# 128-wide stationary reads, a new row order with one store per 128-token tile, and smaller steps in a fused attention and token-mixer kernel

## The chip, the cores and the metric

One core of one Trainium2 chip. The metric is the device time of one execution in microseconds (us). A run is called "slow" when it is over 1.5% above the fastest of its kernel, and the other "fast". A profile is one execution; its span is about 1.8 us shorter than the time of the same run. In the profile PE is TensorE's matmul, PEld its weight load, DVE VectorE, ACT ScalarE, POOL GpSimd, and SP or SyncE the engine that issues most DMAs (93 of 107 before).

## The reference

```python
# q, k, v: (8 batches, 8 heads, 576 tokens, 64); p: (8, 8, 32, 64); fp32 in and out
p_packed = softmax(p @ k.T / 8) @ v               # 32 packed rows a head
x        = softmax(q @ p_packed.T / 8) @ p_packed  # (8, 576, 512) once the heads are side by side
wq, wk   = x @ w_q, x @ w_k                        # (576, 64) each
mixed    = (wq @ wk.T / 8) @ x
out      = relu(mixed) @ w_out                     # (8, 576, 512)
```

## The kernel before

It never builds x: everything after the softmax works with the 512 columns of softmax weights, and each batch goes through 24 kinds of step (transposes of k and q, scores, softmax, `at`, `wk`, `wq`, `g`, `y`, `mx`, `oa`/`ob`). A table of times, `TIMES`, is sorted to give one fixed order of all steps of all batches; each engine runs its part of it in that order. A batch's 576 tokens are token = s * 18 + j, with s from 0 to 31 and j from 0 to 17.

The parts that matter (cuts marked):

```python
def rows(name, b):            # q: partition = (head, s), free = j: 18 tokens next to each other
    ...

def qc(b, c):                 # chunk c takes every third pair of j: j = 6 r + 2 c + x
    ... x_in["q", b].rearrange("a G (r c x) d -> a c G r (x d)", c=NC3, x=2)[:, c]

def sc(b, c):                 # scores: 96 query rows are the stationary operand
    for h in range(H):
        nc.tensor.matmul(ps[:, :, h, :], qT[:, h].rearrange("a r s -> a (r s)"),
                         st[b]["ppT"][:, h], start=True, stop=True)

def wk(b, c):                 # 96 columns of aT are the stationary operand
    ...

def pq(b, _):                 # the first time, it casts the weights itself (DVE and ACT, half each)
    if b == 0:
        for i in range(2):
            copy(i, wqk[:, :, i * Dl:(i + 1) * Dl], w_first[:, :, i * Dl:(i + 1) * Dl])
    ...

def store(b, t0, o):          # a tile of 128 tokens crosses the 96-row pieces: 2 stores a tile
    o_v = out[b].rearrange("(n m) d -> m n d", m=QR)      # QR = 6
    t, end = t0, t0 + o.shape[0]
    while t < end:
        m, n = t // CH, t % CH                            # CH = 96
        k = min(CH - n, end - t)
        nc.sync.dma_start(o_v[m, n:n + k], o[t - t0:t - t0 + k])
        t += k
```

A batch has four tiles of 128 tokens; the last 64 tokens of two batches make up a fifth tile (the "rest").

The softmax here doesn't subtract the row's maximum and nothing guards it: scores larger than these inputs give would overflow.

Of the kernel before, what the change touches and what calls it, by code (L numbers as in the profile page):

```python
# [10 lines left out]
def kernel(  # L11
# [8 lines left out]
    moe_w_out: bass.AP,  # L20
    out: bass.AP,
):



# [10 lines left out]
    nc = tc.nc  # L36
# [21 lines left out]
    NF = KG * RK // NC3  # L58
    NT = NF // 2
    CH = S // (2 * NC3)  # L60
    QR = R // NC3
    VW = Dh + 2
    SM = S // P * P
# [2 lines left out]

    TIMES = (
        (13.00, {
            "lk": (-19.68,),
            "lv": (-16.69,),  # L70
            "lq": (-10.53,),
            "kc": (-1.65, -1.61, -2.24),
            "qc": (4.73, 7.19, 6.10),
            "vc": (1.43, 0.22, 2.76),
            "kt": (0.00, 0.69, 1.45),
            "sa": (1.33, 3.59, 4.04),
            "pv": (6.00,),
            "pb": (23.74,),
            "pt": (8.67,),
            "pq": (16.55,),  # L80
            "qt": (7.33, 11.66, 9.31),
            "sc": (10.66, 13.24, 11.68),
            "sm": (12.44, 14.97, 13.37),
            "at": (18.48, 19.75, 17.43),
            "wk": (20.20, 21.45, 20.93),
            "wq": (22.14, 24.72),
            "g": (22.73,),
            "y": (25.15,),
            "pr": (8.86,),
        }),  # L90
        (13.09, {
            "mx": (30.23, 30.57, 30.04, 33.47, 27.08),
            "oa": (47.09, 37.92, 40.87, 38.92, 43.80),
            "ob": (48.10, 39.32, 41.98, 41.94, 44.92),
        }),
    )

    dve_relu = (0, 1, 0, 0)
    dve_wk = (0, 0, 1)
    dve_wq = (1, 0)  # L100
    dve_out = (0, 0, 1, 0, 0)
    act_kc = (0, 0, 1)
    act_qc = (1, 1, 0)
    act_vc = (0, 0, 1)
    dve_g, dve_y = 1, 0
    def pool(name, bufs, psum=False):
# [10 lines left out]
    def psum(pl, shape, dt, name):  # L117
        return pl.tile(shape, dt, tag="ps", name=name)
# [16 lines left out]
    def load(name, b, pieces=None):  # L135

        x_in[name, b] = t = two.tile(shape[name], fp32, tag=name + "_in", name=name + "_in")
        for o in pieces or [slice(None)]:
            nc.sync.dma_start(t[o], rows(name, b)[o])  # L139
# [17 lines left out]
    wqk = const.tile([Dh, H, 2 * Dl], bf16)  # L157
    wout_w = const.tile([P, NJ, D], bf16)
    ident = const.tile([P, P], bf16)
    w_first = const.tile([Dh, H, 2 * Dl], fp32)  # L160
    warm = const.tile([P, 512], bf16)

    nc.sync.dma_start(p_first, p_v[:, 0])
    by_head = [(slice(None), G) for G in range(KG)]
    load("k", 0, by_head)
    load("v", 0, by_head)
    load("q", 0)
    for i, w in enumerate((moe_w_q, moe_w_k)):
        nc.sync.dma_start(w_first[:, :, i * Dl:(i + 1) * Dl],
                          w.rearrange("(h d) c -> d h c", d=Dh))  # L170
    for name in "kvq":
        load(name, 1)

# [18 lines left out]
    def constants():  # L192
        nc.vector.memset(warm, 0.0)  # L193
        make_identity(nc, ident)
        nc.vector.memset(pT[:, 0:2], 0.0)
        for t in v_bufs:
            nc.vector.memset(t[:, :, Dh:], 1.0)
        for t in ppT_bufs:
            nc.vector.memset(t, 0.0)
        nc.gpsimd.memset(mask, 0.0)  # L200
        for pos in range(NP):
            nc.gpsimd.memset(mask[pos * L:(pos + 1) * L, pos, :], 1.0)
        for t in g_bufs:
            nc.gpsimd.memset(t, 0.0)
        nc.gpsimd.memset(pT[:, 2:], 0.0)
        nc.vector.tensor_copy(
            perm, ident[0:CH, 0:CH].rearrange("a (r sh) -> a sh r", sh=QP))

    def warm_up(n):

        ps = psum(w_pool, [P, 512], fp32, "warm_ps")
        for i in range(n):
            nc.tensor.matmul(ps, warm[:, 0:P], warm, start=True, stop=True)  # L213

    perm = const.tile([CH, QP, NC3], bf16)
    ppT_bufs = [const.tile([P, H, 2, L], bf16, name=f"ppT{i}") for i in range(2)]
    g_bufs = [const.tile([P, NG, P], bf16, name=f"g_sb{i}") for i in range(2)]
    mask = const.tile([P, NP, Dh], fp32)


    st = [{} for _ in range(B)]
# [21 lines left out]
    def qc(b, c):  # L243

        if b < NL:
            st[b]["q", c] = t = three.tile([P, NG, NC3, 2, Dh], bf16, tag="q_c", name="q_c")
            cast(act_qc[c], t.rearrange("a G r x d -> a G r (x d)"),
                 x_in["q", b].rearrange("a G (r c x) d -> a c G r (x d)", c=NC3, x=2)[:, c])

    def kt(b, c):  # L250
        xk = st[b]["k", c] if b < NL else flat(x_in["k", b], c)
# [54 lines left out]
                 ps[r].rearrange("a G (pos l) -> a (G pos) l", l=L))  # L306

    def pq(b, _):
        if b == 0:
            for i in range(2):  # L310
                copy(i, wqk[:, :, i * Dl:(i + 1) * Dl], w_first[:, :, i * Dl:(i + 1) * Dl])
        ps = psum(w_pool, [P, NG, 2 * Dl], fp32, "pqk_ps")
        for h in range(H):
            G, pos = h // NP, h % NP
            nc.tensor.matmul(ps[pos * L:(pos + 1) * L, G, :], st[b]["ppT"][0:Dh, h, 0, :],  # L315
                             wqk[:, h, :], start=True, stop=True)
        st[b]["pqk"] = pqk = three.tile([P, NG, 2 * Dl], bf16, tag="pqk", name="pqk")
        nc.scalar.activation(pqk, ps, COPY)

    def qt(b, c):  # L320
        xq = (st[b]["q", c] if b < NL else
              x_in["q", b].rearrange("a G (r c x) d -> a c G r x d", c=NC3, x=2)[:, c])
        ps = transposes([xq[:, G, r].rearrange("a x d -> a (x d)")
                         for r in range(NC3) for G in range(NG)])
        st[b]["qT", c] = qT = four.tile([P, H, NC3, QP], bf16, tag="qT", name="qT")
        nc.vector.tensor_copy(qT, ps.rearrange("a (r G) (pos s) -> a (G pos) r s", G=NG, s=QP))  # L326

    def sc(b, c):
        qT = st[b]["qT", c]
        ps = psum(sc_pool, [CH, 2, H, L], fp32, "e2_ps")  # L330
        for h in range(H):
            nc.tensor.matmul(ps[:, :, h, :], qT[:, h].rearrange("a r s -> a (r s)"),  # L332
                             st[b]["ppT"][:, h], start=True, stop=True)
        st[b]["e2", c] = e2 = four.tile([CH, 2 * H, L], fp32, tag="e2", name="e2")
        nc.scalar.activation(e2.rearrange("a (x h) l -> a x h l", x=2), ps, EXP, scale=scale)

    def sm(b, c):
        e2 = st[b]["e2", c]
# [6 lines left out]
        st[b]["a2", c] = a2.rearrange("a (x G pos) l -> a x G (pos l)", x=2, G=NG)  # L345

    def at(b, c):
        if "aT" not in st[b]:
            st[b]["aT"] = three.tile([P, NG, NC3, 2, CH], bf16, tag="aT", name="aT")
        ps = psum(tp_pool, [P, NG, 2, CH], bf16, "aT_ps")  # L350
        for par in range(2):
            for G in range(NG):
                nc.tensor.transpose(ps[:, G, par, :], st[b]["a2", c][:, par, G, :],  # L353
                                    perm.rearrange("a s r -> a (s r)"))
        nc.vector.tensor_copy(st[b]["aT"][:, :, c], ps)  # L355

    def wk(b, c):
        ps = psum(w_pool, [CH, 2, Dl], fp32, "wk_ps")
        for par in range(2):
            for G in range(NG):  # L360
                nc.tensor.matmul(ps[:, par, :], st[b]["aT"][:, G, c, par, :],  # L361
                                 st[b]["pqk"][:, G, Dl:], start=G == 0, stop=G == NG - 1)
        st[b]["wk", c] = t = six.tile([CH, 2, Dl], bf16, tag="wk", name="wk")
        copy(dve_wk[c], t, ps)

    def wq(b, half):
        if "wqT" not in st[b]:
            st[b]["wqT"] = four.tile([P, S], bf16, tag="wqT", name="wqT")
        hs = slice(half * S // 2, (half + 1) * S // 2)
        ps = psum(w_pool, [P, S // 2], fp32, "wq_ps")  # L370
        for G in range(NG):
            nc.tensor.matmul(ps, st[b]["pqk"][:, G, :],  # L372
                             st[b]["aT"][:, G].rearrange("a c x s -> a (c x s)")[:, hs],
                             start=G == 0, stop=G == NG - 1)
        if dve_wq[half]:
            nc.vector.tensor_scalar_mul(st[b]["wqT"][:, hs], ps, scale2)
        else:
            nc.scalar.activation(st[b]["wqT"][:, hs], ps, COPY, scale=scale2)

    def g(b, _):  # L380
        ps = psum(w_pool, [P, NG, Dl], fp32, "g_ps")
# [41 lines left out]

    def store(b, t0, o):

        o_v = out[b].rearrange("(n m) d -> m n d", m=QR)
        t, end = t0, t0 + o.shape[0]
        while t < end:
            m, n = t // CH, t % CH
            k = min(CH - n, end - t)  # L430
            nc.sync.dma_start(o_v[m, n:n + k], o[t - t0:t - t0 + k])
            t += k

    def o_half(b, c, half):

# [34 lines left out]
    def lq(b, _):  # L470
        if b >= NL:
            load_cast("q", b)
        if b == NL:
            nc.gpsimd.dma_start(wout_w, moe_w_out.rearrange("(j r) c -> r j c", r=P))

    def pr(b, _):
        if b % 2 == 1 and b + 1 < B:
            p_transposes((b + 1) // 2)

    steps = dict(lk=lk, lv=lv, lq=lq, kc=kc, qc=qc, vc=vc, kt=kt, sa=sa, pv=pv, pb=pb, pt=pt, pq=pq, qt=qt,  # L480
                 sc=sc, sm=sm, at=at, wk=wk, wq=wq, g=g, y=y, mx=mx, oa=oa, ob=ob, pr=pr)
    todo = sorted((t + b * period, b, name, c)
                  for period, times in TIMES for name, ts in times.items()
                  for c, t in enumerate(ts) for b in range(B))
# [40 lines left out]
```

## Time and profile before

| | before |
|---|---|
| time, median of the first 3 runs (range) | 134.47 us (133.61 to 134.76) |
| span of the profiled run | 130.9 us |
| g matmuls of batches 0 to 7 start at | 33.0, 43.9, 56.2, 68.8, 81.2, 93.8, 105.6, 114.8 us |
| start of last matmul to end of span | 6.2 us |
| stores | 72 |

The g matmuls come once a batch; their times are read from the starts of matmuls in the trace.

From the page of the kernel before: busy time of the engines, then the span in 40 slices of 3.3 us (busy tenths of PE; PEclk, the granted clock in tenths; DMA, the mean busy share of 16 DMA engines; GB/s), then the chain of work that ended last, by engine and by line.

```profile
span 130.9 us, 4877 instructions
...
PE 116.0 (89%) x2040; PEld 78.6 (60%) x2040; DVE 80.8 (62%) x198; ACT 86.1 (66%) x176; POOL 67.8 (52%) x90
...
PE   5796299499996999999999999999999999999920
...
PEclk9999859959999999999999999999999999999995
DMA  4999999999999999799999999999953431765784
GB/s 131 323 362 365 262 387 353 322 288 287 275 248 229 343 219 239 121 232 266 406 252 216 291 400 255 201 366 351 189 163 88 111 118 37 222 165 122 227 240 133
...
PE 77%; DMA 7%; ACT 3%; SPq 3%; DVE 2%; issue 2%; POOL 1%; ACTq 0%
PE out_ps L444 24%; PE T_ps L228 12%; DMA q_in<-in_q_dram 7%; PE e_ps L332 7%; PE warm_ps L213 5%; PE mix_ps L413 5%; PE e_ps L265 4%; PE aT_ps L353 4%; PE wk_ps L361 3%; PE pv_ps L280 3%; PE wq_ps L372 3%; SPq L139 3%; PE g_ps L385 2%; PE y_ps L394 1%; PE pqk_ps L315 1%
```

PE is busy to 9 tenths in nearly every slice from the ninth to the 38th, and 77% of the chain is PE. The DMA digits are 9 until slice 29 (but for the first slice and one 7) and then fall: most loads are done by then.

The windows view of a stretch in the middle (length, then busy time and count of each engine, clock, DMA share, GB/s):

```profile
core 0: us, PE busy (x) PEld busy (x) DVE busy (x) ACT busy (x) POOL busy (x), PEclk, DMA share, GB/s
...
61.60:74.00 12.40, 12.40 (x249) 8.99 (x247) 9.53 (x23) 9.67 (x22) 7.25 (x10) 1.00 1.09 290
...
```

PE is busy for all of the stretch and the others for 58 to 78% of it.

Groups of instructions (line, engine, operation, operands, shape, count | busy us, mean ns of one | idle time of the engine before them, and its releaser):

```profile
L124 ACT ACTIVATE o_sb<-out_ps 128x512 f32<-128x512 f32 x28 | 16.7, 595 | 7.7 <-PE out_ps L444 6.0 <-ACT wk L124 0.6 <-DMA out_dram<-o_sb 0.6
...
L332 PEld LDWEIGHTS <-qT 128*96 128x96 bf16 x192 | 11.6, 128 | 1.3 <-issue 0.2
L444 PEld LDWEIGHTS <-relu 128*128 128x128 bf16 x128 | 11.2, 99 | 7.4 <-issue 0.4
...
L361 PEld LDWEIGHTS <-aT 128*96 128x96 bf16 x96 | 7.0, 124 | 2.2 <-DVE aT L355 0.2
```

A weight load of 96 columns takes 128 or 124 ns and one of 128 columns 99 ns, although it loads more.

DMA issues of stores (out, in, queue, count, KB each, median us from issue to landing):

```profile
out_dram<-o_sb SPq DMA_DIRECT2D x24, 192.0 KB, 3.7
...
out_dram<-o_sb SPq DMA_DIRECT2D x24, 64.0 KB, 3.4
```

They land in 3.4 to 3.7 us (medians) for 64 to 192 KB. Two lines of the timeline of the end (start, duration, engine, what):

```profile
118.08 10.21 SPq L431 DMA_DIRECT2D out_dram<-o_sb  x18
...
125.20 0.60 ACT L124 ACTIVATE o_sb<-out_ps 128x512 f32<-128x512 f32 x1 [0.31 <-PE out_ps L444]
```

SyncE issues the last 18 stores back to back until 128.3 us, while the last tile is copied at 125.2 to 125.8.

### The profile page before, as it was taken

To read this page: it belongs to the slowest core of one execution; us is meant where nothing else is said; L and a number is where in the kernel's file an instruction comes from. 1 tells how busy PE (TensorE), PEld (TensorE's weight loads), DVE (VectorE), ACT (ScalarE), POOL (GpSimd) and SP (SyncE) were. 2 spreads that over 40 slices of the span, in tenths; PEclk is the share of its full clock that TensorE was granted. 3 is DMA by queue.
4 is the path that set the end of the run, shared out by engine and by line. 5 is a ranking of instruction groups with operands and counts; after the bars stand their busy time and mean duration, and the time that the engine had idled before them with its cause. 6 is when DMAs were issued, how large, how long until landed. Compare 5 with 4: busy or idle time off the path is not lost.

```text
span 130.9 us, 4877 instructions
## 1 busy us (share of the span) xinstructions
PE 116.0 (89%) x2040; PEld 78.6 (60%) x2040; DVE 80.8 (62%) x198; ACT 86.1 (66%) x176; POOL 67.8 (52%) x90
## 2 busy tenths in 40 slices
PE   5796299499996999999999999999999999999920
PEld 1253277257864975786678677767876785654400
DVE  6150049526796877878777887887688777524200
ACT  3144426572794689588867877696789678858530
POOL 7924527994099268709841982388048408400000
PEclk9999859959999999999999999999999999999995
DMA  4999999999999999799999999999953431765784
GB/s 131 323 362 365 262 387 353 322 288 287 275 248 229 343 219 239 121 232 266 406 252 216 291 400 255 201 366 351 189 163 88 111 118 37 222 165 122 227 240 133
DMA packets 18630, 32.10 MB, mean 245 GB/s; under 512 B 2736, under 2 KB 6832, under 8 KB 18608
## 3 DMA queue, kind: packets, MB, share of 16 engines
q1 hardware_dynamic: 12880, 23.99, 55.1%
q0 software_dynamic: 5728, 7.80, 35.4%
q8 instruction: 16, 0.26, 0.8%
q14 instruction: 6, 0.05, 0.1%
HBM read 30.15 MB, written 9.44 MB: 302 GB/s over the span
## 4 chain that ended last, share of the span: by engine, by line
PE 77%; DMA 7%; ACT 3%; SPq 3%; DVE 2%; issue 2%; POOL 1%; ACTq 0%
PE out_ps L444 24%; PE T_ps L228 12%; DMA q_in<-in_q_dram 7%; PE e_ps L332 7%; PE warm_ps L213 5%; PE mix_ps L413 5%; PE e_ps L265 4%; PE aT_ps L353 4%; PE wk_ps L361 3%; PE pv_ps L280 3%; PE wq_ps L372 3%; SPq L139 3%; PE g_ps L385 2%; PE y_ps L394 1%; PE pqk_ps L315 1%
## 5 line engine op out<-in xcount | busy, mean ns | idle before, releaser
L444 PE MATMUL out_ps<-wout_w,relu 128*128 128x512 bf16 x128 | 33.9, 379 | 0.0
L124 ACT ACTIVATE o_sb<-out_ps 128x512 f32<-128x512 f32 x28 | 16.7, 595 | 7.7 <-PE out_ps L444 6.0
L326 DVE COPY qT<-T_ps 128x768 bf16<-128x768 bf16 x24 | 13.3, 555 | 9.7 <-PE T_ps L228 9.3
L213 PE MATMUL warm_ps<-warm 128*128 128x512 bf16 x40 | 17.5, 472 | 1.2 <-DVE warm L193 1.2
L255 DVE COPY kT<-T_ps 128x768 bf16<-128x768 bf16 x24 | 13.0, 546 | 6.7 <-PE T_ps L228 5.7
L444 PEld LDWEIGHTS <-relu 128*128 128x128 bf16 x128 | 11.2, 99 | 7.4 <-issue 0.4
L404 ACT ACTIVATE relu<-mix_ps 128x512 bf16<-128x512 f32 x24 | 13.5, 604 | 2.7 <-PE mix_ps L413 2.4
L332 PEld LDWEIGHTS <-qT 128*96 128x96 bf16 x192 | 11.6, 128 | 1.3 <-issue 0.2
L355 DVE COPY aT<-aT_ps 128x384 bf16<-128x384 bf16 x24 | 8.5, 353 | 6.2 <-PE aT_ps L353 6.2
L413 PE MATMUL mix_ps<-wqT,y 128*128 128x512 bf16 x32 | 10.6, 381 | 0.1
L294 POOL TENSOR_TENSOR ppb<-pp,mask 128x256 bf16<-128x256 bf16 x16 | 10.5, 676 | 0.1
L228 PE MATMUL T_ps<-ident,q_bf 128*128 128x128 bf16 x108 | 9.1, 219 | 1.1 <-issue 1.1
L122 DVE COPY o_sb<-out_ps 128x512 f32<-128x512 f32 x8 | 5.4, 671 | 7.1 <-PE out_ps L444 3.7
L228 PE MATMUL T_ps<-ident,k_bf 128*128 128x128 bf16 x108 | 9.0, 219 | 0.0
L265 PE MATMUL e_ps<-pT,kT 128*64 128x64 bf16 x288 | 8.3, 201 | 0.2 <-DVE kT L255 0.2
L228 PEld LDWEIGHTS <-k_bf 128*128 128x128 bf16 x108 | 7.0, 98 | 2.2
L361 PEld LDWEIGHTS <-aT 128*96 128x96 bf16 x96 | 7.0, 124 | 2.2 <-DVE aT L355 0.2
L124 ACT ACTIVATE wk<-wk_ps 96x128 bf16<-96x128 f32 x16 | 4.3, 270 | 6.0 <-PE wk_ps L361 6.0
L228 PEld LDWEIGHTS <-q_bf 128*128 128x128 bf16 x108 | 7.0, 100 | 2.0 <-issue 1.5
L265 PEld LDWEIGHTS <-kT 128*64 128x64 bf16 x288 | 6.2, 113 | 3.3 <-DVE kT L255 1.1
L361 PE MATMUL wk_ps<-pqk,aT 128*96 128x64 bf16 x96 | 7.7, 207 | 0.0
L342 DVE RECIPROCAL rr<-rs 96x16 f32<-96x16 f32 x24 | 6.0, 249 | 1.8
(320 smaller groups left out, 272.2 us busy)
## 6 DMA issues: line engine op xcount, KB each, us to landing
v_in<-in_v_dram SPq DMA_DIRECT2D x7, 1152.0 KB, 10.0
out_dram<-o_sb SPq DMA_DIRECT2D x24, 192.0 KB, 3.7
k_bf<-in_k_dram POOLq DMA_DIRECT2D x6, 576.0 KB, 11.7
q_bf<-in_q_dram POOLq DMA_DIRECT2D x6, 576.0 KB, 8.2
out_dram<-o_sb SPq DMA_DIRECT2D x24, 128.0 KB, 3.5
q_in<-in_q_dram SPq DMA_DIRECT2D x2, 1152.0 KB, 12.8
out_dram<-o_sb SPq DMA_DIRECT2D x24, 64.0 KB, 3.4
k_in<-in_k_dram SPq DMA_DIRECT2D x4, 288.0 KB, 3.7
```

The lines of the kernel that those rows point to most:

```text
L124: nc.scalar.activation(o, i, COPY)
L213: nc.tensor.matmul(ps, warm[:, 0:P], warm, start=True, stop=True)
L228: nc.tensor.transpose(ps[:, t, :], block, ident)
L255: nc.vector.tensor_copy(kT, ps)
L265: nc.tensor.matmul(ps[m, t], kT[:, t, m], heads[:, 2 * h0:2 * h1 + 2:2 * (h1 - h0) + 1], start=True, stop=True)
L294: nc.gpsimd.tensor_tensor(ppb[:, G], st[b]["pp"][:, G, 0:1, :].to_broadcast((P, NP, Dh)), mask, op=MULT)
L326: nc.vector.tensor_copy(qT, ps.rearrange("a (r G) (pos s) -> a (G pos) r s", G=NG, s=QP))
L332: nc.tensor.matmul(ps[:, :, h, :], qT[:, h].rearrange("a r s -> a (r s)"), st[b]["ppT"][:, h], start=True, stop=True)
L361: nc.tensor.matmul(ps[:, par, :], st[b]["aT"][:, G, c, par, :], st[b]["pqk"][:, G, Dl:], start=G == 0, stop=G == NG - 1)
L404: nc.scalar.activation(o, i, RELU)
L413: nc.tensor.matmul(ps, yT[:, j * P:(j + 1) * P], wqT[:, 0:SM], start=True, stop=True)
L444: nc.tensor.matmul(ps, lhsT, wout_w[:, j, :], start=j == 0, stop=j == NJ - 1)
```

## The change

Its intent: read the weights of scores and wk 128 wide (the 32 columns too many belong to the next head or a zero pad, and their results are never read), so that the load takes the 99 ns of a 128-column one and not 124 to 128; choose rows so that 128 tokens of out are one regular DMA; make wq per chunk, so that it needn't wait for a half; cast the small weights as steps of their own, and load them before q. The order of steps was fitted anew.

```diff
-            cast(... x_in["q", b].rearrange("a G (r c x) d -> a c G r (x d)", c=NC3, x=2)[:, c])
+            cast(... x_in["q", b].rearrange("a G (c r x) d -> a c G r (x d)", c=NC3, x=2)[:, c])
# scores, and wk in the same way; qT and aT become fixed buffers with a zero pad of 32 columns
-        ps = psum(sc_pool, [CH, 2, H, L], fp32, "e2_ps")
+        ps = psum(sc_pool, [P, 2, H, L], fp32, "e2_ps")
         for h in range(H):
-            nc.tensor.matmul(ps[:, :, h, :], qT[:, h].rearrange("a r s -> a (r s)"),
+            nc.tensor.matmul(ps[:, :, h, :], qT[:, h * CH:h * CH + P],
                              st[b]["ppT"][:, h], start=True, stop=True)
# wq: 3 chunks of 192 columns in place of 2 halves of 288; all on ACT; one more relu on DVE
# weights: loaded into output buffers before q, and cast in steps "wc" on ACT; q of batch 0 in 3 loads
     def store(b, t0, o):
-        o_v = out[b].rearrange("(n m) d -> m n d", m=QR)
-        t, end = t0, t0 + o.shape[0]
-        while t < end:
-            m, n = t // CH, t % CH
-            k = min(CH - n, end - t)
-            nc.sync.dma_start(o_v[m, n:n + k], o[t - t0:t - t0 + k])
-            t += k
+        n = o.shape[0] // QP                                      # QP = 32
+        nc.sync.dma_start(
+            out[b].rearrange("(s j) d -> j s d", j=R)[t0 // QP:t0 // QP + n],   # R = 18
+            o)
# ... (TIMES, the engine of each eviction and of some casts, and the operand of the warm-up matmuls changed too)
```

More of the change, by code (lines that the diff above doesn't have):

```diff
@@ L60 @@
     CH = S // (2 * NC3)
+    PAD = P - CH
     QR = R // NC3
@@ L68 @@
         (13.00, {
-            "lk": (-19.68,),
-            "lv": (-16.69,),
-            "lq": (-10.53,),
-            "kc": (-1.65, -1.61, -2.24),
-            "qc": (4.73, 7.19, 6.10),
-            "vc": (1.43, 0.22, 2.76),
-            "kt": (0.00, 0.69, 1.45),
-            "sa": (1.33, 3.59, 4.04),
-            "pv": (6.00,),
-            "pb": (23.74,),
-            "pt": (8.67,),
-            "pq": (16.55,),
-            "qt": (7.33, 11.66, 9.31),
-            "sc": (10.66, 13.24, 11.68),
-            "sm": (12.44, 14.97, 13.37),
-            "at": (18.48, 19.75, 17.43),
-            "wk": (20.20, 21.45, 20.93),
-            "wq": (22.14, 24.72),
-            "g": (22.73,),
-            "y": (25.15,),
-            "pr": (8.86,),
-        }),
-        (13.09, {
-            "mx": (30.23, 30.57, 30.04, 33.47, 27.08),
-            "oa": (47.09, 37.92, 40.87, 38.92, 43.80),
-            "ob": (48.10, 39.32, 41.98, 41.94, 44.92),
+            "lk": (-20.02,),
+            "lv": (-16.79,),
+            "lq": (-9.81,),
+            "kc": (-3.51, -0.84, -2.25),
+            "qc": (5.53, 6.68, 5.38),
+            "vc": (-0.49, 2.31, 2.35),
+            "kt": (0.00, 1.68, 1.54),
+            "sa": (1.39, 3.02, 2.92),
+            "pv": (5.79,),
+            "pb": (23.13,),
+            "pt": (7.81,),
+            "pq": (14.00,),
+            "qt": (9.65, 10.22, 6.81),
+            "sc": (12.18, 12.94, 9.66),
+            "sm": (13.07, 15.48, 12.14),
+            "at": (18.57, 19.72, 16.97),
+            "wk": (19.93, 22.49, 20.85),
+            "wq": (22.64, 25.47, 25.97),
+            "g": (23.46,),
+            "y": (26.35,),
+            "pr": (9.83,),
+            "wc": (9.00, 9.50),
+        }),
+        (13.11, {
+            "mx": (29.53, 29.32, 29.98, 28.93, 35.84),
+            "oa": (46.33, 41.06, 42.47, 39.49, 43.39),
+            "ob": (48.09, 41.28, 42.65, 41.28, 44.75),
         }),
     )
-    dve_relu = (0, 1, 0, 0)
+    dve_relu = (0, 1, 0, 1)
     dve_wk = (0, 0, 1)
-    dve_wq = (1, 0)
+    dve_wq = (0, 0, 0)
     dve_out = (0, 0, 1, 0, 0)
-    act_kc = (0, 0, 1)
-    act_qc = (1, 1, 0)
+    act_kc = (0, 1, 0)
+    act_qc = (0, 1, 1)
     act_vc = (0, 0, 1)
@@ L159 @@
     ident = const.tile([P, P], bf16)
-    w_first = const.tile([Dh, H, 2 * Dl], fp32)
-    warm = const.tile([P, 512], bf16)
+    warm = const.tile([P, P], bf16)
     nc.sync.dma_start(p_first, p_v[:, 0])
@@ L166 @@
     load("v", 0, by_head)
-    load("q", 0)
+    w_first = []
     for i, w in enumerate((moe_w_q, moe_w_k)):
-        nc.sync.dma_start(w_first[:, :, i * Dl:(i + 1) * Dl],
-                          w.rearrange("(h d) c -> d h c", d=Dh))
+        t = opool.tile([P, D], fp32, tag="o", name="w_first")[0:Dh].rearrange(
+            "a (h c) -> a h c", c=Dl)
+        nc.sync.dma_start(t, w.rearrange("(h d) c -> d h c", d=Dh))
+        w_first.append(t)
+    load("q", 0, [(slice(None), slice(None), slice(c * QR, (c + 1) * QR)) for c in range(NC3)])
     for name in "kvq":
@@ L205, in constants @@
         nc.gpsimd.memset(pT[:, 2:], 0.0)
-        nc.vector.tensor_copy(
-            perm, ident[0:CH, 0:CH].rearrange("a (r sh) -> a sh r", sh=QP))
+        for t in qT_bufs:
+            nc.vector.memset(t[:, H * CH:], 0.0)
+        for t in aT_bufs:
+            nc.vector.memset(t[:, :, NG * CH:], 0.0)
     def warm_up(n):
@@ L212, in warm_up @@
         for i in range(n):
-            nc.tensor.matmul(ps, warm[:, 0:P], warm, start=True, stop=True)
-    perm = const.tile([CH, QP, NC3], bf16)
+            nc.tensor.matmul(ps.rearrange("a (x n) -> a x n", n=P), warm,
+                             warm.unsqueeze(1).to_broadcast((P, 4, P)), start=True, stop=True)
+    qT_bufs = [const.tile([P, H * CH + PAD], bf16, name=f"qT{i}") for i in range(4)]
+    aT_bufs = [const.tile([P, 2 * NC3, NG * CH + PAD], bf16, name=f"aT{i}") for i in range(3)]
     ppT_bufs = [const.tile([P, H, 2, L], bf16, name=f"ppT{i}") for i in range(2)]
@@ L218 @@
     mask = const.tile([P, NP, Dh], fp32)
+    qt_order = sorted(range(NC3), key=lambda c: TIMES[0][1]["qt"][c])
+    qt_order = [qt_order.index(c) for c in range(NC3)]
     st = [{} for _ in range(B)]
@@ L247, in qc @@
             cast(act_qc[c], t.rearrange("a G r x d -> a G r (x d)"),
-                 x_in["q", b].rearrange("a G (r c x) d -> a c G r (x d)", c=NC3, x=2)[:, c])
+                 x_in["q", b].rearrange("a G (c r x) d -> a c G r (x d)", c=NC3, x=2)[:, c])
     def kt(b, c):
@@ L308, in pq @@
     def pq(b, _):
-        if b == 0:
-            for i in range(2):
-                copy(i, wqk[:, :, i * Dl:(i + 1) * Dl], w_first[:, :, i * Dl:(i + 1) * Dl])
         ps = psum(w_pool, [P, NG, 2 * Dl], fp32, "pqk_ps")
@@ L321, in qt @@
         xq = (st[b]["q", c] if b < NL else
-              x_in["q", b].rearrange("a G (r c x) d -> a c G r x d", c=NC3, x=2)[:, c])
+              x_in["q", b].rearrange("a G (c r x) d -> a c G r x d", c=NC3, x=2)[:, c])
         ps = transposes([xq[:, G, r].rearrange("a x d -> a (x d)")
                          for r in range(NC3) for G in range(NG)])
-        st[b]["qT", c] = qT = four.tile([P, H, NC3, QP], bf16, tag="qT", name="qT")
-        nc.vector.tensor_copy(qT, ps.rearrange("a (r G) (pos s) -> a (G pos) r s", G=NG, s=QP))
+        st[b]["qT", c] = qT = qT_bufs[(NC3 * b + qt_order[c]) % 4]
+        nc.vector.tensor_copy(
+            qT[:, 0:H * CH].rearrange("a (h r s) -> a h r s", r=NC3, s=QP),
+            ps.rearrange("a (r G) (pos s) -> a (G pos) r s", G=NG, s=QP))
     def sc(b, c):
         qT = st[b]["qT", c]
-        ps = psum(sc_pool, [CH, 2, H, L], fp32, "e2_ps")
+        ps = psum(sc_pool, [P, 2, H, L], fp32, "e2_ps")
         for h in range(H):
-            nc.tensor.matmul(ps[:, :, h, :], qT[:, h].rearrange("a r s -> a (r s)"),
+            nc.tensor.matmul(ps[:, :, h, :], qT[:, h * CH:h * CH + P],
                              st[b]["ppT"][:, h], start=True, stop=True)
         st[b]["e2", c] = e2 = four.tile([CH, 2 * H, L], fp32, tag="e2", name="e2")
-        nc.scalar.activation(e2.rearrange("a (x h) l -> a x h l", x=2), ps, EXP, scale=scale)
+        nc.scalar.activation(e2.rearrange("a (x h) l -> a x h l", x=2), ps[0:CH], EXP,
+                             scale=scale)
     def sm(b, c):
@@ L347, in at @@
     def at(b, c):
-        if "aT" not in st[b]:
-            st[b]["aT"] = three.tile([P, NG, NC3, 2, CH], bf16, tag="aT", name="aT")
-        ps = psum(tp_pool, [P, NG, 2, CH], bf16, "aT_ps")
+        aT = aT_bufs[b % 3]
+        ps = psum(tp_pool, [P, 2, NG, CH], bf16, "aT_ps")
         for par in range(2):
             for G in range(NG):
-                nc.tensor.transpose(ps[:, G, par, :], st[b]["a2", c][:, par, G, :],
-                                    perm.rearrange("a s r -> a (s r)"))
@@ L355, in at @@
-        nc.vector.tensor_copy(st[b]["aT"][:, :, c], ps)
+                nc.tensor.transpose(ps[:, par, G, :], st[b]["a2", c][:, par, G, :],
+                                    ident[0:CH, 0:CH])
+        nc.vector.tensor_copy(aT[:, 2 * c:2 * c + 2, 0:NG * CH],
+                              ps.rearrange("a x G s -> a x (G s)"))
     def wk(b, c):
-        ps = psum(w_pool, [CH, 2, Dl], fp32, "wk_ps")
+        aT = aT_bufs[b % 3]
+        ps = psum(w_pool, [P, 2, Dl], fp32, "wk_ps")
         for par in range(2):
@@ L360, in wk, with wq @@
             for G in range(NG):
-                nc.tensor.matmul(ps[:, par, :], st[b]["aT"][:, G, c, par, :],
+                nc.tensor.matmul(ps[:, par, :], aT[:, 2 * c + par, G * CH:G * CH + P],
                                  st[b]["pqk"][:, G, Dl:], start=G == 0, stop=G == NG - 1)
         st[b]["wk", c] = t = six.tile([CH, 2, Dl], bf16, tag="wk", name="wk")
-        copy(dve_wk[c], t, ps)
-    def wq(b, half):
+        copy(dve_wk[c], t, ps[0:CH])
+    def wq(b, c):
         if "wqT" not in st[b]:
@@ L368, in wq @@
             st[b]["wqT"] = four.tile([P, S], bf16, tag="wqT", name="wqT")
-        hs = slice(half * S // 2, (half + 1) * S // 2)
-        ps = psum(w_pool, [P, S // 2], fp32, "wq_ps")
+        ps = psum(w_pool, [P, 2 * CH], fp32, "wq_ps")
         for G in range(NG):
-            nc.tensor.matmul(ps, st[b]["pqk"][:, G, :],
-                             st[b]["aT"][:, G].rearrange("a c x s -> a (c x s)")[:, hs],
-                             start=G == 0, stop=G == NG - 1)
-        if dve_wq[half]:
-            nc.vector.tensor_scalar_mul(st[b]["wqT"][:, hs], ps, scale2)
+            nc.tensor.matmul(
+                ps.rearrange("a (r x s) -> a r x s", r=NC3, s=QP), st[b]["pqk"][:, G, :],
+                aT_bufs[b % 3][:, 2 * c:2 * c + 2, G * CH:(G + 1) * CH].rearrange(
+                    "a x (r s) -> a r x s", s=QP),
+                start=G == 0, stop=G == NG - 1)
@@ L377, in wq @@
+        o = st[b]["wqT"][:, c * 2 * CH:(c + 1) * 2 * CH]
+        if dve_wq[c]:
+            nc.vector.tensor_scalar_mul(o, ps, scale2)
         else:
-            nc.scalar.activation(st[b]["wqT"][:, hs], ps, COPY, scale=scale2)
+            nc.scalar.activation(o, ps, COPY, scale=scale2)
     def g(b, _):
@@ L474, in lq, with wc @@
             nc.gpsimd.dma_start(wout_w, moe_w_out.rearrange("(j r) c -> r j c", r=P))
+    def wc(b, i):
+        if b == 0:
+            copy(False, wqk[:, :, i * Dl:(i + 1) * Dl], w_first[i])
     def pr(b, _):
@@ L480 @@
     steps = dict(lk=lk, lv=lv, lq=lq, kc=kc, qc=qc, vc=vc, kt=kt, sa=sa, pv=pv, pb=pb, pt=pt, pq=pq, qt=qt,
-                 sc=sc, sm=sm, at=at, wk=wk, wq=wq, g=g, y=y, mx=mx, oa=oa, ob=ob, pr=pr)
+                 sc=sc, sm=sm, at=at, wk=wk, wq=wq, g=g, y=y, mx=mx, oa=oa, ob=ob, pr=pr, wc=wc)
     todo = sorted((t + b * period, b, name, c)
```

## The prediction

> **What bounds the kernel now.** TensorE. By the windows view PE is busy for the whole of every stretch from 49 to 111 us (DVE, ACT and POOL 60 to 82%), and the chain of waits is 77% PE. From the starts of matmuls in the trace one batch takes about 12.4 us (the g matmuls come at 56.4, 69.0 and 81.4), of which only some 0.7 us are gaps over 40 ns. Before about 37 us it waits on loads, casts and latency. After the last matmul (125.1 us) there are another 5.8 us.
>
> **Removed, term by term.**
>
> 1. Scores (L332, 192 matmuls) and wk (L361, 96) load 96-column weights. The groups show 128 and 124 ns for such a load and 98 to 101 ns for a 128-column one. Start to start, both come every 45 ns; the g matmuls, with the same 64 moving columns but 128 weight columns, every 29 ns. [...] So 16 ns each: 36 x 16 = 0.58 us a batch. Six score batches and about seven wk batches run where PE is the bound: 3.4 to 3.7 us, nearly all on the path. The period should become about 11.8 us.
>
> 2. Stores: 72 become 36. At the end SyncE issues 18 stores back to back from 118.1 to 128.3 us, the last starting 127.9 although its tile was ready at 125.8. With one store per tile the last should issue right after the copy. I estimate last matmul to end at about 4.2 us (0.7 copy, 2.7 store, 0.85 closing) in place of 5.8: 1.5 us.
>
> 3. Start: pq waits 1.67 us for the DVE cast of the weights (24.66 us, on the chain). As own steps on ACT it should be gone. But the 1024 packets of 256 B (about 20 ns each, and DMA fell to 160 GB/s around them) now come before q, and the q third that is used first (c = 2) lands last; before, q landed at 14.6 us. I expect the first q transposes 0 to 0.7 us later, pq 1 to 1.5 us earlier; net 0.5 to 1 us.
>
> **Neutral.** wq: 48 matmuls of 192 columns (estimate 83 ns) for 32 of 288 (123 ns): 0.50 us a batch both ways. Evictions: ACT gains three of about 325 ns (between 270 for 128 and 384 for 256 columns), loses one of 399 and one relu of 604: 0. DVE gains a relu of 687 and loses 456: +0.2 us a batch, not the bound. New waits from the shifted order of steps: 0.5 to 1 us in all.
>
> **Prediction.** 3.6 + 1.5 + 0.7 - 0.6 = 5.2 us: 129.2 us, range 126.8 to 132.0. Faster by over 2%: 0.88; within 2%: 0.10; slower: 0.02.
>
> **What would show it.** Scores and wk start every 28 to 30 ns, their loads take about 98 ns; period 11.7 to 11.9 us; SyncE issues the last store within 0.3 us of its tile; no DVE weight cast ahead of pq; PE still busy all through the middle.
>
> **What would make it wrong.** The 128-wide read not being fast; the strided moving operand of wq being slow; new waits in the new order (score PSUM freed by ACT, aT by DVE) making the period 12.2 or more; loads, whose slack at batch 2 is only 3 us, becoming the bound once PE is faster; a slower start because q comes later.

(One sentence of term 1 is cut out. It held no term of the sum, which stays 3.6 + 1.5 + 0.7 - 0.6 = 5.2 us; the 16 ns are the measured 45 ns less the measured 29. Where its estimates come from, as far as the trace of the kernel before shows: the packets of 256 B take a median of 18 ns, and from 13 to 14 us DMA moves 161 GB/s; 83 ns for 192 columns lies on the line through 123 ns at 288 columns and 216 ns at 512; 0.85 us is about the time from SyncE's last wait for a semaphore, at 130.0 us, to the end at 130.9; the 2.7 us of a store are an estimate, the 72 stores land 1.8 to 7.3 us after their issue, median 3.5.)

## More of the kernel before

`o` comes from a pool of five buffers, `opool`.

## The result, and the profile after

| | before | after |
|---|---|---|
| time, median (range) | 134.22 us of 4 runs (133.61 to 134.76) | 191.35 us of 4 runs (190.99 to 193.64) |
| ratio of the fast runs | | 1.429 (95%: 1.416 to 1.443) |
| span of the profiled run | 130.9 us | 189.2 us |
| mean granted clock | 0.964 | 0.840 |
| stores | 72 | 40 |

A ratio here is the mean time of one kernel's fast runs over that of the other's of the same rounds, so it is not quite the ratio of the medians.

The page after:

```profile
span 189.2 us, 4853 instructions
...
PE 120.2 (64%) x2039; PEld 80.4 (42%) x2057; DVE 84.4 (45%) x203; ACT 85.1 (45%) x185; POOL 67.6 (36%) x90
...
PE   3783998979999950886508991399895752910000
...
PEclk9997599999999995599955999579999998585555
DMA  5999999999969992228942882212222222222110
GB/s 183 350 264 389 361 306 347 231 223 287 191 139 242 255 219 74 87 106 188 284 134 101 281 185 76 102 65 100 101 94 99 92 80 83 102 102 102 65 71 29
...
DMA 57%; PE 23%; ACT 5%; DVE 3%; issue 2%; SPq 2%; ACTq 0%; DVEq 0%
DMA out_dram<-o_sb 50%; PE T_ps L240 5%; DMA q_in<-in_q_dram 4%; PE warm_ps L220 4%; DMA v_in<-in_v_dram 3%; PE e_ps L343 2%; PE out_ps L456 2%; ACT o_sb L127 2%; PE g_ps L400 2%; PE e_ps L277 2%; PE pv_ps L292 1%; PE mix_ps L428 1%; PE wq_ps L384 1%; PE aT_ps L364 1%; SPq L142 1%
```

PE is busy as long in total (120 us for 116) but now over 189 us, and its granted clock falls to 5 tenths around its gaps (slices 16 and 17, 21 and 22, and the last four). The chain has moved from PE to DMA, half of it stores. And the rows of DMA and GB/s show how: over the last third of the span the 16 engines are busy to 2 tenths, at about 100 GB/s. Yet 57% of the chain is DMA. I took this to mean that only a part of the 16 engines was in use.

Groups, after (as above):

```profile
L127 ACT ACTIVATE o_sb<-out_ps 128x512 f32<-128x512 f32 x28 | 16.4, 596 | 55.4 <-DMA out_dram<-o_sb 49.8 <-PE out_ps L456 5.2 <-ACT v_bf_83 L151 0.5
...
L456 PEld LDWEIGHTS <-relu 128*128 128x128 bf16 x128 | 11.9, 102 | 19.0 <-issue 11.1
...
L374 PEld LDWEIGHTS <-aT_121 128*128 128x128 bf16 x36 | 1.8, 98 | 2.0 <-issue 1.8
```

The 128-wide read worked: the loads of L374 take 98 ns for 124 before. But the copies out of PSUM to `o_sb` on ACT have 55.4 us of idle time in front of them, 49.8 for stores still reading the buffer.

The waits (who waited for whom: us in total, times, longest):

```profile
ACT o_sb L127 <- DMA out_dram<-o_sb: 49.8, 14, 8.0
...
PE g_ps L400 <- ACT o_sb L127: 19.8, 3, 7.1
...
DVE o_sb L125 <- DMA out_dram<-o_sb: 15.0, 2, 12.6
```

The chain in order of time (start, duration, what):

```profile
55.70 19.57 DMA out_dram<-o_sb
75.38 0.61 ACT o_sb L127
76.03 0.80 PE g_ps L400 x12
...
79.39 19.40 DMA out_dram<-o_sb
98.89 0.61 ACT o_sb L127
...
103.88 16.75 DMA out_dram<-o_sb
```

A store takes 12 to 20 us; an `o_sb` buffer comes free; ACT copies one tile; PE, which waits for that PSUM bank, runs a few matmuls; and the next store is waited for.

DMA issues, after:

```profile
out_dram<-o_sb SPq DMA_DIRECT2D x32, 256.0 KB
...
k_bf<-in_k_dram POOLq DMA_DIRECT2D x6, 576.0 KB, 14.6
...
out_dram<-o_sb SPq DMA_DIRECT2D x8, 128.0 KB
```

The stores have no time to landing any more. The view gives one where a semaphore has 16 increments for every DMA issued on it; k_bf, issued by POOL, has one.

Three counts from the trace led to the theory. Its records of semaphore increments hold 1488 for SyncE's 93 DMAs before, 16 each. After, SyncE has 63 DMAs; if the 23 loads still give 16 each, the 40 stores give 552 - 368 = 184, which is 32 x 5 + 8 x 3. The store's new pattern is 4 x 32 x 512 (2 x 32 x 512 for a rest), so 5 and 3 are one more than its outermost dimension; what the one more is was not shown. (The stores before had 96, 64 or 32 rows outermost, with 16 increments each.) Second, a packet of 2 KB takes a median of 84 ns before and after. Third, packets of stores in flight: 4.0 in mean from 126 to 131 us and 4.2 from 140 to 150, in place of 8.9 from 126 to 131 before.

So theory 1, at this point my estimate from these counts: the stores run on k = 4 (rests: 2) DMA engines of 16, always the same ones, and those before on k = 16. The records do not name a packet's engine. Rivals: (2) one store per tile is too coarse for five buffers; (3) the DRAM rows of a store, now 18 x 2 KB = 36 KB apart where they were 12 KB apart, are slow to write.

### The profile page after: what moved, and what is told of

Same layout as the page of the kernel before. It is cut to its first block, busy times and chain, and to the rows that moved or that the text cites. A ratio compares the mean times of both kernels' runs of the same rounds, so it can differ in the third digit from the quotient of the medians.

```text
span 189.2 us, 4853 instructions
## 1 busy us (share of the span) xinstructions
PE 120.2 (64%) x2039; PEld 80.4 (42%) x2057; DVE 84.4 (45%) x203; ACT 85.1 (45%) x185; POOL 67.6 (36%) x90
## 4 chain that ended last, share of the span: by engine, by line
DMA 57%; PE 23%; ACT 5%; DVE 3%; issue 2%; SPq 2%; ACTq 0%; DVEq 0%
DMA out_dram<-o_sb 50%; PE T_ps L240 5%; DMA q_in<-in_q_dram 4%; PE warm_ps L220 4%; DMA v_in<-in_v_dram 3%; PE e_ps L343 2%; PE out_ps L456 2%; ACT o_sb L127 2%; PE g_ps L400 2%; PE e_ps L277 2%; PE pv_ps L292 1%; PE mix_ps L428 1%; PE wq_ps L384 1%; PE aT_ps L364 1%; SPq L142 1%
## 5 line engine op out<-in xcount | busy, mean ns | idle before, releaser
L127 ACT ACTIVATE o_sb<-out_ps 128x512 f32<-128x512 f32 x28 | 16.4, 596 | 55.4 <-DMA out_dram<-o_sb 49.8
L456 PE MATMUL out_ps<-wout_w,relu 128*128 128x512 bf16 x118 | 35.1, 402 | 4.8 <-ACT o_sb L127 3.6
L456 PEld LDWEIGHTS <-relu 128*128 128x128 bf16 x128 | 11.9, 102 | 19.0 <-issue 11.1
L417 DVE TENSOR_SCALAR relu<-mix_ps 128x512 bf16<-128x512 f32 x16 | 10.3, 682 | 6.8 <-PE mix_ps L428 4.4
L428 PE MATMUL mix_ps<-wqT,y 128*128 128x512 bf16 x26 | 9.5, 379 | 4.2 <-ACT o_sb L127 3.4
L419 ACT ACTIVATE relu<-mix_ps 128x512 bf16<-128x512 f32 x16 | 9.4, 601 | 2.4 <-PE mix_ps L428 2.0
L125 DVE CAST g_sb_127<-g_ps 128x128 bf16<-128x128 f32 x4 | 1.2, 290 | 15.9 <-PE g_ps L400 15.9
L240 PEld LDWEIGHTS <-k_bf 128*128 128x128 bf16 x108 | 7.6, 108 | 0.5
L393 ACT ACTIVATE wqT<-wq_ps 128x192 bf16<-128x192 f32 x24 | 7.7, 326 | 0.1
L153 POOL CAST v_bf_82<-v_in 128x768 bf16<-128x768 f32 x6 | 4.9, 823 | 3.8 <-DMA v_in<-in_v_dram 3.8
L356 POOL TENSOR_TENSOR a_2290<-e_2242,rr 96x512 bf16<-96x512 f32 x1 | 1.0, 1043 | 14.2 <-DVE rr L354 14.2
```

What stands on the lines that cost most here:

```text
L125: nc.vector.tensor_copy(o, i)
L127: nc.scalar.activation(o, i, COPY)
L240: nc.tensor.transpose(ps[:, t, :], block, ident)
L393: nc.scalar.activation(o, ps, COPY, scale=scale2)
L417: nc.vector.tensor_scalar_max(o, i, 0.0)
L419: nc.scalar.activation(o, i, RELU)
```

## The experiments

"Before" runs beside each: medians 134.3 to 135.1 us. Ratios are to the kernel before, with their 95% intervals.

### e1: s outermost in the store

```diff
# relu (and the rest's relu) writes its tokens as (s, j) in place of (j, s):
-            relu(dve_relu[j], st[b]["relu"][:, j], ps)
+            relu(dve_relu[j], st[b]["relu"][:, j].rearrange("a (t s x) -> a t x s", x=4, s=QP),
+                 ps.rearrange("a (t x s) -> a t x s", x=4, s=QP))
-            out[b].rearrange("(s j) d -> j s d", j=R)[t0 // QP:t0 // QP + n],
+            out[b].rearrange("(s j) d -> s j d", j=R)[:, t0 // QP:t0 // QP + n],
```

> The changed kernel, but relu writes its tokens as (s, j) and the one store of a tile has 32 rows of s outermost and then 4 adjacent rows of j (each 8 KB in one piece in DRAM). Same number of stores (40 issues), same bytes, no wider relu. Theory 1 (a store whose slowest dimension is 4 or 2 runs on 4 or 2 of the 16 DMA engines): the slowest dimension is now 32, so 16 engines; the stores overlap again, mean time of a 2 KB packet stays 84 to 100 ns, and the kernel takes 127 to 132 us. Rival 2 (one store per tile is too large a unit for five o_sb buffers): still over 170 us. Rival 3 (the DRAM rows are too far apart, 36 KB, for writes): fast too, since four rows are now adjacent; the per-j run tells that one from theory 1.

Measured: 135.52 us median of 4, ratio 1.011 (1.001 to 1.021). The same 40 stores of the same size no longer hold anything up, so rival 2 falls. But it is not the 127 to 132 us expected. Groups of e1:

```profile
L417 DVE TENSOR_SCALAR relu<-mix_ps 128x512 bf16<-128x512 f32 x16 | 19.7, 1315 | 5.7 <-PE mix_ps L428 5.7
...
L419 ACT ACTIVATE relu<-mix_ps 128x512 bf16<-128x512 f32 x16 | 19.7, 1367 | 2.2 <-PE mix_ps L428 2.2
```

And of its view of DMA issues (size in KB, median time from issue to landing in us):

```profile
out_dram<-o_sb SPq DMA_DIRECT2D x32, 256.0 KB, 3.3
```

The stores land in 3.3 us. The relu, however, which I had thought free of cost, doubled: 1315 ns on DVE and 1367 on ACT, for 682 and 601 in the changed kernel. Its bf16 writes now step by 8 bytes, in a pattern of more dimensions; no run parts the two. With four relus a batch this adds about 2.8 us of DVE and ACT work to each, and the chain shows relu at 11%. My edit had brought a cost of its own, so this run settles the store but not the rest.

### e2: the same rows in twice as many stores, two j each

```diff
-        nc.sync.dma_start(out[b].rearrange("(s j) d -> j s d", j=R)[t0 // QP:t0 // QP + n], o)
+        o_v = out[b].rearrange("(s j) d -> j s d", j=R)
+        for i in range(0, n, 2):
+            nc.sync.dma_start(o_v[t0 // QP + i:t0 // QP + i + 2], o[i * QP:(i + 2) * QP])
```

> The changed kernel, but each tile stored by two DMAs of 2 x 32 rows in place of one of 4 x 32: same rows, same DRAM addresses, 72 stores instead of 40. Theory 1: each runs on 2 engines, always the same two, so those two carry 4608/2 = 2304 packets of 84 ns = 194 us after the first store at about 50 us, plus their share of the loads (about 30 us): 255 to 285 us, DMA share near 0.13 in the tail, about 50 GB/s. Rivals 2 and 3: no slower than the changed kernel (191 us) or faster, since pieces are smaller and the addresses are the same.

Measured: 273.49 us median of 2, ratio 2.038 (2.006 to 2.070). Smaller pieces of the same rows made it 82 us slower than the change, as theory 1 had it; both rivals had it equal or better. The page of e2 (DMA share in tenths, GB/s):

```profile
DMA  6999999967915156151651111111111111111110
GB/s 223 265 381 331 333 222 243 176 114 121 173 41 202 52 109 129 44 205 54 122 195 54 52 55 51 53 51 51 51 54 51 51 51 51 51 51 51 51 51 37
```

A plateau of 51 GB/s, half of the 102 of the changed kernel, at a DMA share of 1 tenth.

### e3: one store per j

```diff
+        for i in range(n):
+            nc.sync.dma_start(o_v[t0 // QP + i], o[i * QP:(i + 1) * QP])
```

> The changed kernel, but each tile stored by four DMAs of 32 rows (one j each): same rows, same 36 KB row distance in DRAM, 144 stores. Theory 1: slowest dimension 32, 16 engines, the stores no longer bound: 129 to 137 us, what is left being SyncE, which needs about 0.45 us per store (65 us in all, at the end 16 to 20 of them back to back, so a tail of 2 to 6 us longer than with one store). Rival 3 (distance of rows in DRAM): stays near 190 us. Rival 2 (unit too large): fast too; e1 tells that one from theory 1.

Measured: 148.36 us median of 4, ratio 1.104 (1.093 to 1.116): 43 us faster than the change, with the same rows 36 KB apart, so rival 3 falls. The size of what is left was a miss (129 to 137 expected). The trace gives the reason: the 144 stores begin every 0.48 us (median), 69 us in all; from 122.7 us SyncE issues them nearly back to back, and the chain runs through its issues; the last matmul starts at 131.0 us and the span ends at 147.7. I had allowed 16 to 20 stores in a row at the end; there were over 40.

### e4 and e6: the kernel before with 128-wide reads alone

```diff
# on the kernel before; wk and aT likewise; wq reads the new aT layout in the old halves;
# the weights of pq lie in output buffers, as in the change, so that it fits
-            nc.tensor.matmul(ps[:, :, h, :], qT[:, h].rearrange("a r s -> a (r s)"),
+            nc.tensor.matmul(ps[:, :, h, :], qT[:, h * CH:h * CH + P],
```

> The kernel before with one thing of the change alone: weights of scores and wk read 128 wide (padded fixed buffers for qT and aT; wq reads the new aT layout in the old halves; the weights of pq lie in output buffers so that it fits). Old row order, stores, casts and order of steps. My prediction's first term: pitch of scores and wk 45 to 29 ns, 0.58 us a batch, 3.4 to 3.7 us in all: 130.3 to 131.5 us, ratio 0.969 to 0.978. A rival (the saving is off the path or given back in waits): within 1 us of before.

Three of the 4 runs of e4, the profiled one among them, were slow (its fast run: 130.84 us). It was run again with 5 rounds:

> The same kernel as e4, whose runs were nearly all called slow (one fast run at 130.8 us; its g matmuls from batch 0 to 7 took 78.7 us, before 81.8). Term 1 alone: 3.1 to 3.7 us below before, ratio 0.970 to 0.980, if the start is not slower. Rival: within 1%.

Measured (e6): 132.66 us median of 6, before 134.32; the ratio of fast runs is 0.998 (0.990 to 1.007), because one of the 11 runs of before was as low as 131.81 us and only four counted as fast. So in the total it is not resolved, and the expectation failed. In the profile the term is there: scores and wk start every 29 ns (median) in place of 45, and from g of batch 3 to g of batch 6 a batch takes 12.02 us for 12.26. But g of batch 0 came at 35.5 us for 33.0. What that extra start comes from in this run is open; it differs from run to run of one kernel (37.8 us in e4, the same kernel).

### e5: every fourth token as weights, so that the store has 16 outermost

Reordering on the weight side instead would leave relu alone. With the order (s, j), two steps on the stationary operand, the kernel did not build. But with one step of 4 the 128 columns of a tile come out as 16 j by 8 s, and by theory 1 an outermost dimension of 16 is enough.

```diff
-            lhsT = (st[b]["relu"][:, j, c * P:(c + 1) * P] if c < NJ
+            lhsT = (st[b]["relu"][:, j, c::NJ] if c < NJ                # NJ = 4
-    def store(b, t0, o): ...
+    def store(b, c, o):
+        nc.sync.dma_start(
+            out[b].rearrange("(u t j) d -> t j u d", t=NJ, j=R)[c, 0:SM // QP], o)   # 16 x 8 x 512
# a rest: two stores of 32 rows, one for each j
```

> The changed kernel with stores on 16 engines and without the dearer relu of e1 (there the permuted write took 1.32 to 1.37 us in place of 0.6 to 0.69 and cost some 2.8 us of DVE and ACT a batch): a tile of out takes every fourth token column as weights, so its store is 16 j outermost, then 8 rows; the rests are stored as two DMAs of 32 rows. All else as changed. If the store was the whole loss and my terms were right: relu back at 0.60 and 0.69 us, period 11.8 to 12.0 us, last matmul to end about 4.8 us as in e1, 127.5 to 131 us, ratio 0.945 to 0.975. Rival (the new order of steps gives the gain back in waits): 132 to 135 us, with waits of 0.5 us and more in the middle.

Measured: 130.39 us median of 6, ratio 0.975 (0.963 to 0.987). Groups of e5:

```profile
L460 PEld LDWEIGHTS <-relu 128*128 128x128 bf16 x128 | 13.0, 113 | 8.3 <-issue 0.6
...
L417 DVE TENSOR_SCALAR relu<-mix_ps 128x512 bf16<-128x512 f32 x16 | 10.3, 682 | 5.7 <-PE mix_ps L428 5.7
...
L419 ACT ACTIVATE relu<-mix_ps 128x512 bf16<-128x512 f32 x16 | 9.4, 599 | 3.1 <-PE mix_ps L428 2.9
```

The relu is back at 682 and 599 ns. The weight load with step 4 takes 113 ns for 102 in the changed kernel, behind matmuls that start every 216 ns, so it cost nothing here. Everything but the stores is as in the change: with stores of 16 outermost it takes 61 us less, and is faster than the kernel before. From batch 3 to 6 a batch takes 11.88 us (12.26 before), as predicted. The end did not get shorter: 6.1 us from the last matmul (6.2 before).

### e7 and e8: the start

e7 loads the weights after q, as before; e8 also loads q of batch 0 in one piece.

```diff
-    (weights)                         +    load("q", 0, three pieces)     # e8: load("q", 0)
-    load("q", 0, three pieces)        +    (weights)
```

> e5 with the weights loaded after q again, q still in three pieces. My third term said that the 1024 packets of 256 B ahead of q delay the first q transposes by up to 0.7 us: then those come 0.5 to 1.5 us earlier than in e5 and the kernel is 0 to 1 us faster; pq does not wait for the weights as its place is some 7 us later. Rival (the start is bound by loads of batch 1, not by q): no change, within 0.5 us of e5.

Measured (e7): 132.32 us median of 6, ratio 0.993 (0.985 to 1.002); e5 in the same rounds 0.975. The first q cast did come earlier (11.7 us for 14.0), but g of batch 0 at 37.6 us for 33.3: the v of batch 1 came later (its casts began at 26.4 us for 24.3), and two softmax steps of batch 0 follow it on POOL. Both expectations missed. That the new order of loads did this is not shown: e10 (below), whose start is e5's line for line, has these casts at 26.4 us and g of batch 0 at 37.7 in its profile (a run called slow).

> e7 with q of the first batch in one load again. If the three pieces help (first piece cast early): 0 to 1 us slower than e7. As the piece used first by PE is the one landing last (c = 2), I expect no difference over 0.5 us.

Measured (e8): 131.01 us median of 4 (129.54 to 134.01), of which two were slow. The order of the first loads is not resolved by these runs; that the start is set by loads of the next batches, not by q or by pq, fits e5, e7 and the chain of e5 (below).

### e9 and e10: how many engines, dosed

The rows, addresses and row order of e5, each tile's store split into four DMAs (4 x 8 rows, k = 4) or two (8 x 8, k = 8). By theory 1 all four DMAs of a tile in e9 run on the same four engines, the "those" of its expectation.

```diff
+        o_v = out[b].rearrange("(u t j) d -> t j u d", t=NJ, j=R)
+        for i in range(0, 16, 4):                       # e10: 8
+            nc.sync.dma_start(o_v[c, i:i + 4], o[i * 8:(i + 4) * 8])
```

> e5 (130.4 us) with each tile's store split into four DMAs of 4 x 8 rows: same rows, addresses, packet size and row order, four times as many stores. Theory 1: [...] those carry 1024 packets of a tile store each (86 us) and 3 us of rests after about 49 us, and some 36 us as their share of the loads that run then: 165 to 182 us, with a plateau of about 98 GB/s at the end. If the address pattern or the size of one store had been the cause in the changed kernel, this stays at e5 plus a SyncE tail of some 6 us: 131 to 140 us.

Measured (e9): 176.39 us median of 2, ratio 1.317 (1.304 to 1.330). Windows of its end, after PE's last stretch:

```profile
core 0: us, PE busy (x) PEld busy (x) DVE busy (x) ACT busy (x) POOL busy (x), PEclk, DMA share, GB/s
140.00:160.00 20.00, 10.03 (x53) 4.93 (x50) 2.96 (x5) 6.57 (x15) 0.00 (x0) 0.93 0.30 104
160.00:174.00 14.00, 0.00 (x0) 0.00 (x0) 0.00 (x0) 0.60 (x1) 0.00 (x0) 0.50 0.29 98
```

About 100 GB/s at a DMA share of 0.3, from a kernel whose addresses run at 130 us when not split. The number of stores is not the cause: e3 also issues 144 stores of 64 KB, with 32 rows outermost, and takes 148 us.

> e5 with two DMAs of 8 x 8 rows a tile: 8 engines. They carry 43 + 3 us of stores and 36 us of loads after 49 us: about 131 us if never idle, so just at the limit of the 130 us of e5: 131 to 143 us; stores land later than in e5 and o_sb copies begin to wait for them. If only 16 engines or few matter without a sum behind it, it would be half-way between e5 and e9.

Measured (e10): 140.93 us median of 4, ratio 1.044 (1.033 to 1.054); inside the range, with a slow profile. 

All five kernels together. The estimate is worked out from traces, on theory 1: the first store begins at 49.8 us; the busiest engine then moves n packets of 84 ns; and its share of the loads that run after that is 36.8 us (the durations of all other packets after 50.4 us in the changed kernel's trace, over 16). It leaves out any time in which that engine has nothing to do, which is one candidate for the 6 us that e10 is over it; no run settles that.

| run | store dimensions | n on the busiest engine | 49.8 + n x 0.084 + 36.8 | measured |
|---|---|---|---|---|
| e2 | 2 x 32 | 2304 | 280 us | 273.0 us (span) |
| after | 4 x 32, rests 2 x 32 | 1280 | 194 us | 189.2 us (span) |
| e9 | 4 x 8, rests 32 | 1056 | 175 us | 174.8 us (span) |
| e10 | 8 x 8, rests 32 | 544 | 132 us | 137.9 and 138.1 us (spans of its fast runs) |
| e5 | 16 x 8, rests 32 | 288 | 111 us | 128.7 us (span): PE is the bound |

Two counts from the traces fit the same numbers of engines without any sum of times. The most frequent number of store packets in flight at once is 2 in e2 (90% of 180 to 260 us), 4 in the changed kernel (75% of 126 to 160 us) and in e9 (73% of 152 to 173 us), 8 in e10 (41% of 126 to 144 us) and 16 in e5 (25% of 118 to 127 us). The four DMAs of a tile in e9 together had no more in flight than one store of the changed kernel, which fits "always the same ones"; which engines they are was not shown. And with 368 semaphore increments taken off for the 23 loads, what is left for the stores is 216 = 72 x 3 in e2, 896 = 128 x 5 + 16 x 16 in e9 and 832 = 64 x 9 + 16 x 16 in e10: k + 1 for each store with k under 16, and 16 for each rest of 32 rows.

### e11 and e12: the end, and one cast

e11 is e8 with two of the last four rest stores issued by POOL; e12 also makes the first cast of p on ACT.

```diff
+            queue = nc.gpsimd if b >= B - 2 and i == 1 else nc.sync
+            queue.dma_start(o_v[SM // QP + i], o[i * QP:(i + 1) * QP])
# e12:
-            nc.vector.tensor_copy(p_nat[:, 0], p_first)
+            copy(False, p_nat[:, 0], p_first)
```

> e8 (w after q, q in one load) with two of the last four rest stores issued by POOL, which is idle then. In e5 the last tile was ready at 123.6 us and its store began at 124.9, as SyncE still issued four rest stores of 0.42 to 0.6 us. Last matmul to end 6.1 to 5.1 us, so 129.5 to 130.5 us median and 3 to 4% under before; if the landing of the rests, not SyncE, sets the end: no change from e8 (131.0).

Measured (e11): 131.93 us median of 6, ratio 0.980 (0.970 to 0.990). The last store now begins 0.3 us after its tile (1.3 in e5), yet the end takes 6.5 us: the last four stores land between 127.6 and 128.9 us, 3.5 to 4.1 us after their issue. The rival reading, that landing and not SyncE sets the end here, is the one that held.

> e11 with the first cast of p on ACT in place of DVE. In some profiles (after, e5 to e8) that cast took 2.8 us on DVE beside a POOL memset, in others (before, e1, e4) 0.3 us, and the first kT copy came at 9.3 instead of 7.1 us. If this matters for the start: 0.3 to 1 us below e11 in the median and less spread. If loads of batch 1 set the start anyway: no change (within 0.5 us).

Measured (e12): 130.13 us median of 6 (129.51 to 131.32), ratio 0.973 (0.966 to 0.980), all six fast. The cast, in the changed kernel:

```profile
L185 DVE CAST p_nat<-p_first 128x256 bf16<-128x256 f32 x1 | 2.9, 2868 | 0.1
```

The same view of e12:

```profile
L127 ACT ACTIVATE p_nat<-p_first 128x256 bf16<-128x256 f32 x1 | 0.4, 416 | 0.9 <-DMA p_first<-in_p_dram 0.9
```

On DVE it ran beside a POOL memset of 2.66 us and took 2.87 us; the first kT copy came at 9.3 us, in e12 at 6.9. In e12 the cast on ACT took 0.42 us and the same memset again 2.66 us. In the profiles of before, e1 and e4 the same cast on DVE beside the same memset took 0.3 us, and the memset 2.80 to 2.87 us. The cast began first in both kinds: 0.10 us ahead of the memset in before, 0.13 in e1, 0.06 in the changed kernel. That the memset held up the cast in the changed kernel is my estimate, from two durations that are nearly the same; what decides it was not shown. e12 has the best interval of all, but its gap to e5 (0.3 us of medians, in other rounds) is below what these runs resolve. Against e11, in the same rounds, its median is 1.8 us lower, more than the 0.3 to 1 us expected, but their intervals overlap and g of batch 0 comes no earlier (32.4 us for 32.2), so that the cast did this is not shown.

## Why the prediction was wrong, point by point

- **Term 2, the stores, is the step that failed.** "With one store per tile the last should issue right after the copy", with "2.7 store", costed a store by its issue on SyncE and took the landing from stores of another shape. (The count was off as well: 40, not 36, as a rest needs two.) The runs showed in its place: stores of 4 x 32 rows had 4 packets of 2 KB in flight (75% of 126 to 160 us), 84 ns each, as on 4 DMA engines where packets queue one behind the other; after the first store at 49.8 us, 1280 such packets plus that engine's loads make about 194 us by the estimate, for 189.2 measured. At the same rows, a smaller outermost dimension made it worse (2 in e2 for 4 in the change, 273 us for 191; 4 and 8 in e9 and e10 for 16 in e5, 176 and 141 for 130) and one of 32 removed it (e3 against the change, 148 us for 191); e1 and e5 removed it with other rows. The shape 4 x 32 x 512 could be read off the program beforehand; what it costs was shown by these runs. In my list of what would make the prediction wrong, no store appears.
- **Term 1, 128-wide weights, had the right mechanism.** Loads 124 to 98 ns, pitch 45 to 29 ns. The size in the middle is nearly right: e5 takes 11.88 us a batch from batch 3 to 6 where 11.8 was predicted.
- **Term 1 does not pay in the first three batches.** g of batch 2 comes at 56.4 us in e5 and 56.2 before. The chain of e5 (start, duration, what) shows the bound there:

```profile
26.89 1.04 POOL a L356
...
30.16 15.54 DMA k_bf<-in_k_dram
45.74 0.51 PE T_ps L240 x6
```

  POOL issues a load of k at 30.2 us behind its other work, and PE starts from its landing at 45.7. This is the item "loads ... becoming the bound once PE is faster" of my list, and it came true in batches 0 to 2. The profile shows it; no run isolated it. e12, with g of batch 0 a microsecond earlier than e5 (32.4 us), has g of batch 2 at 56.4 again.
- **Term 3, the start**: the wait of pq did go (pq begins at 22.7 us in e5 for 25.1), but g of batch 0 stayed at 33.3 us. Other waits are there in e5: POOL waits 0.8 us for v of batch 1, and PE 1.1 us for ACT's cast of q; which of them holds g was not isolated. Gain 0 in these two profiles for the 0.5 to 1 us predicted, where g of batch 0 varies by as much with the same start (33.3 us in e5, 32.3 in e9).
- **Neutral items** held: wq's matmuls start every 83 ns (estimate 83), its eviction takes 326 ns (estimate 325).
- **The end without the fault**: 4.8 us in e1 (4.2 estimated), but 6.1 in e5 and e12 and 6.5 in e11, so the 1.5 us are not certain with a correct store either.
- **The sum.** With the store repaired the predicted 5.2 us became about 2.2 in the spans of the profiles (130.9 and 128.7), all of it after g of batch 2 (58.6 to 56.2 us until g of batch 7); the medians of the same rounds differ by 3.9 us (134.3 and 130.4). The predicted 129.2 us lies 1.2 us under e5's median.

## What to carry to other kernels

When a change merges DMAs, look at the outermost dimension of the merged pattern on both sides: stores on SyncE's queue with an outermost dimension of 2, 4 or 8 most often had that many packets in flight here (e2, the changed kernel and e9, e10), whether they had 64, 128 or 256 KB, and took 273, 191 and 176, and 141 us where 16 outermost took 130 (e5). In the profile it showed as a mean DMA share of 0.1 and 51 GB/s at 2 (e2) and of 0.2 to 0.3 and about 100 GB/s at 4 (the changed kernel and e9), with a chain that is 57% DMA and no time to landing in the view of issues (the changed kernel). Compute the work of the busiest engine, not the mean (by the estimate above 194 us for 189.2 measured). A step on the weight side of a matmul, hidden behind a 512-column stream, can be the cheapest place to reorder rows (e5: loads of 113 ns for 102, behind matmuls 216 ns apart); a reorder in the eviction doubled its time here (e1: 1315 ns for 682 on DVE, 1367 for 601 on ACT).
